# Part of an attention kernel's exponentials moved to VectorE, and some score matmuls made dense

## The chip, the cores and the metric

One core of a Trainium2 chip. The metric is the device time of one execution in microseconds (us), lower is better. Each run also has the mean clock that TensorE was granted, as a share of full speed, and a state: fast or slow (slow is over 1.5% above the fastest of the same kernel in its call). PE is TensorE, PEld its weight loads, DVE is VectorE, ACT is ScalarE, POOL is GpSimd.

## The reference, cut to what matters

Two independent layers on 2048 positions of width 448, 16 heads of 28, their outputs side by side.

```python
def _A_ref(x, wq, wk, wv, wo):          # first attention: all heads share one k and one v
    q = heads(x @ wq); k = x @ wk; v = x @ wv
    scores = einsum("bhqd,bkd->bhqk", q, k) * Dh ** -0.5
    return merge(einsum("bhqk,bkd->bhqd", softmax(scores), v)) @ wo
def _B_ref(x, wqkv, wo):                # second attention: each query sees 8 keys, 2 apart
    ...                                 # gather k and v at pos, pos-2, .. pos-14, softmax over 8
```

The first has 16 x 2048 x 2048 exponentials. The second has few, but many elementwise products.

## The kernel before: the parts that matter

A small scheduler in the program orders every instruction of each engine in advance from assumed durations; on the chip each engine gets its list in that order and waits on semaphores. The scores of the first attention come in 1024 units of one bank of PSUM, the memory that all 3821 matmuls in the trace of before write to (`ps`; 128 keys x 512 queries), four heads row-tiled in TensorE's array (the score matmuls of one batch start 3 ns apart there, in the median). ScalarE exponentiates them in batches of three and two banks in turn (`SLOTS`):

```python
for i, (sc, t, tb, j) in enumerate(us):                       # scores, 32 rows of the array each
    r = e.matmul(g.bank(b0 + i), g.kT[32*j:32*j+32, 128*tb:128*tb+128],
                 g.qT[32*j:32*j+32, sc % 2, t, :], start=True, stop=True, tile_position=(32*j, 0))
...
x = a("act", t_exp(w), lambda e, b0=b0, w=w, n=n: e.activation(
    g.expT[:, n % ERING, 0:w], g.ps[:, 512*b0:512*b0+w], ACT.Exp, scale=SCALE),
  R=[("ring", slot)], W=[("expT", n % ERING)], pr=-50)
...
for (sc, t, tb, j), r, i in grp:                              # value products, four units at a time
    x = e.matmul(g.bank(PVBANK, p0=32*j, p1=32*j+32), g.v_aug[:, tb, :],
                 g.expT[:, r, 512*i:512*i+512], start=tb == 0, stop=tb == 15, tile_position=(0, 32*j))
```

Sixteen key blocks of four heads (a "quad") accumulate in one bank; VectorE copies it out and normalises. The second attention runs in the gaps: its products on VectorE, its sums over TensorE. Where TensorE has had little dense work lately, by the scheduler's count (`area`), it puts matmuls on a tile of zeros ("fillers"): ahead of scores, ahead of small sums, or in idle time.

## Time and profile before

| | before |
|---|---|
| time, median of the first 3 executions | 502.77 us (500.17 to 507.64) |
| the profiled execution | 499.83 us, clock 0.996 |
| ScalarE busy | 476.4 us of 497.9 |
| VectorE busy | 237.6 us |
| exponentials | 205 of three banks, 204 of two, 1 of one |

The page and its groups are read in the prediction. What it tells but does not show is how the room on VectorE is spread. Busy time by stretch, before; the first columns are the stretch and its length, then each engine's busy us (count), last the granted clock, the share of the DMA engines and GB/s:

```profile
60.00:180.00 120.00, 116.07 (x988) 46.55 (x985) 64.16 (x118) 118.53 (x106) 3.40 (x5) 1.00 0.16 52
...
420.00:480.00 60.00, 57.16 (x448) 20.77 (x446) 18.48 (x35) 59.87 (x55) 1.23 (x2) 1.00 0.10 32
```

The third busy time, 64.16 of 120 us, is VectorE's: half busy in the middle, and less at the end.

### The profile page before, as it was taken

What the parts mean: (1) busy time and instruction counts of PE and PEld (TensorE: products, weight loads), DVE (VectorE), ACT (ScalarE), POOL (GpSimd) and SP (SyncE); (2) the same over time, 40 slices, a digit from 0 to 9 for tenths busy, and PEclk for the clock granted to TensorE, in tenths of its full rate; (3) what the DMA queues carried; (4) which work ended last, traced back from release to release, by engine and by line L of the source; (5) the groups of instructions that cost most, each with busy time, mean ns of one, the idle gap of its engine ahead of it and who ended that gap; (6) DMA issues with size and microseconds to landing.
All of it is one profiled execution on the core that took longest, in us unless ns stands there. A gap on an engine that the chain in (4) does not pass through costs nothing.

```text
span 497.9 us, 8754 instructions
## 1 busy us (share of the span) xinstructions
PE 477.7 (96%) x3821; PEld 185.1 (37%) x3821; DVE 237.6 (48%) x443; ACT 476.4 (96%) x431; POOL 25.3 (5%) x47
## 2 busy tenths in 40 slices
PE   8999999999989999999999999999999999999996
PEld 3433434343343334434343333434433343333322
DVE  3236448744463357454942495256722564037202
ACT  3989999999999999999999999999999999999994
POOL 8020000000000000000000000000000000000000
PEclk9989999999999999999999999999999999999999
DMA  7880220022003120302011302120020302020001
GB/s 158 146 229 2 84 73 13 18 84 84 1 11 108 34 73 11 93 0 84 1 41 62 121 2 67 37 66 19 20 84 18 103 11 94 0 84 1 20 0 38
DMA packets 41590, 27.35 MB, mean 55 GB/s; under 512 B 17058, under 2 KB 41040, under 8 KB 41552
## 3 DMA queue, kind: packets, MB, share of 16 engines
q1 hardware_dynamic: 39600, 25.65, 17.9%
q10 hardware_dynamic: 1776, 0.81, 0.6%
q8 instruction: 30, 0.49, 0.4%
q0 software_dynamic: 176, 0.33, 0.2%
q14 instruction: 8, 0.07, 0.0%
HBM read 17.60 MB, written 5.52 MB: 46 GB/s over the span
## 4 chain that ended last, share of the span: by engine, by line
ACT 62%; PE 31%; DVE 4%; DMA 1%; issue 1%; ACTq 0%
ACT expT L711 61%; PE ps L699 8%; PE ps L821 6%; PE ps L724 5%; PE ps L651 2%; PE ps L837 2%; DVE prod L915 2%; PE ps L697 1%; PE ps L749 1%; PE ps L926 1%; DMA wq<-in_A_wq_dram 1%; PE ps L933 1%; PE ps L780 1%; PE ps L665 1%; DVE a_n L902 1%
## 5 line engine op out<-in xcount | busy, mean ns | idle before, releaser
L711 ACT ACTIVATE expT<-ps 128x1536 bf16<-128x1536 f32 (+1 forms) x410 | 469.2, 1268 | 7.3 <-PE ps L699 6.0
L699 PE MATMUL ps<-qT,kT 32*128 32x512 bf16 x1024 | 160.2, 386 | 6.8 <-ACT expT L711 3.5
L724 PE MATMUL ps<-expT,v_aug 128*32 128x512 bf16 x1024 | 102.3, 390 | 0.4 <-DVE PV_sb L744 0.4
L699 PEld LDWEIGHTS ps<-qT,kT 32*128 32x128 bf16 x1024 | 39.3, 91 | 104.1 <-ACT expT L711 61.3
L724 PEld LDWEIGHTS ps<-expT,v_aug 128*32 128x32 bf16 x1024 | 26.2, 93 | 58.4 <-issue 55.9
L821 PE MATMUL ps<-xT_B,wqkv 128*112 128x512 bf16 (+1 forms) x128 | 44.9, 408 | 0.3 <-DVE qTB L827 0.3
L341 PE MATMUL ps<-warm 128*128 128x512 bf16 x140 | 42.9, 383 | 0.6 <-DVE rden L755 0.6
L862 DVE TENSOR_TENSOR stage<-qTB,kTB 112x1024 bf16<-112x1024 bf16 x64 | 41.5, 689 | 0.1
L915 DVE TENSOR_TENSOR prod<-Vsh,a_n 128x896 bf16<-128x896 bf16 x64 | 38.6, 658 | 0.0
L757 POOL COPY rrep<-rden 128x512 bf16<-128x512 bf16 x15 | 10.4, 695 | 419.0 <-DVE rden L755 419.0
L883 DVE TENSOR_REDUCE mx<-ps 128x16 f32<-128x128 f32 x15 | 4.4, 291 | 54.2 <-PE ps L871 54.2
L697 PE MATMUL ps<-warm 128*128 128x512 bf16 x69 | 25.7, 389 | 4.3 <-ACT expT L711 3.5
L871 PE MATMUL ps<-ones,stage 112*128 112x4 bf16 x512 | 28.2, 168 | 0.0
L871 PEld LDWEIGHTS ps<-ones,stage 112*128 112x128 bf16 x512 | 23.1, 96 | 13.3 <-issue 8.2
L926 PE MATMUL ps<-ident,padd 128*112 128x128 bf16 x256 | 25.5, 228 | 0.2
L364 PE MATMUL ps<-warm 128*128 128x384 bf16 x78 | 24.1, 328 | 0.5 <-DVE PV_sb L744 0.5
L926 PEld LDWEIGHTS ps<-ident,padd 128*112 128x112 bf16 x256 | 18.2, 129 | 12.1 <-issue 8.6
L821 PEld LDWEIGHTS ps<-xT_B,wqkv 128*112 128x112 bf16 (+1 forms) x128 | 14.4, 127 | 22.1 <-issue 18.9
L744 DVE COPY PV_sb<-ps 128x512 f32<-128x512 f32 x15 | 10.4, 691 | 25.2 <-PE ps L724 25.2
L651 PE MATMUL ps<-xT_A,wq 128*128 128x512 bf16 x64 | 20.9, 395 | 0.1
L755 DVE RECIPROCAL rden<-ps 128x16 bf16<-128x16 f32 x16 | 4.1, 253 | 34.3 <-PE ps L749 34.3
L749 PEld LDWEIGHTS ps<-sel,PV_sb 128*128 128x128 f32 x128 | 18.5, 190 | 5.1 <-issue 3.8
(97 smaller groups left out, 344.1 us busy)
## 6 DMA issues: line engine op xcount, KB each, us to landing
Vsh<-v_scratch SPq DMA_DIRECT2D x16, 896.0 KB, 4.6
v_scratch<-Vst SPq DMA_DIRECT2D x16, 112.0 KB, 1.7
out_dram<-outB SPq DMA_DIRECT2D x16, 112.0 KB, 1.7
out_dram<-outA SPq DMA_DIRECT2D x14, 112.0 KB, 1.7
wqkv<-in_B_wqkv_dram SPq DMA_DIRECT2D x1, 1008.0 KB, 5.6
stage<-in_A_x_dram ACTq DMA_DIRECT2D x1, 448.0 KB, 3.5
wo_B<-in_B_wo_dram SPq DMA_DIRECT2D x4, 98.0 KB
wo<-in_A_wo_dram SPq DMA_DIRECT2D x4, 98.0 KB
```

The costliest lines, as they stand in the source:

```text
L341: self.s.FILL = lambda b: (lambda e: e.matmul(self.bank(b), self.warm[:, 0:128], self.warm[:, :], start=True, stop=True))
L364: eng.matmul(self.bank(o.use.bank, 512 - lo, lo), self.warm[:, 0:128], self.warm[:, lo:512], start=True, stop=True)
L651: a("pe", t_mm(512), lambda e, u=u, t=t, kt=kt: e.matmul(g.bank(u.bank), g.wq4[64 * (kt // 3):, t, kt, :], g.xT_A[64 * (kt // 3):, kt, 512 ...
L697: e.matmul(g.bank(b0), g.warm[:, 0:128], g.warm[:, :], start=True, stop=True)
L699: r = e.matmul(g.bank(b0 + i), g.kT[32 * j:32 * j + 32, 128 * tb:128 * tb + 128], g.qT[32 * j:32 * j + 32, sc % 2, t, :], start=True, stop ...
L711: x = a("act", t_exp(w), lambda e, b0=b0, w=w, n=n: e.activation(g.expT[:, n % ERING, 0:w], g.ps[:, 512 * b0:512 * b0 + w], ACT.Exp, scale ...
L724: x = e.matmul(g.bank(PVBANK, p0=32 * j, p1=32 * j + 32), g.v_aug[:, tb, :], g.expT[:, r, 512 * i:512 * i + 512], start=tb == 0, stop=tb = ...
L821: a("pe", t_mm(512), lambda e, u=u, t=t, kt=kt, w=w: e.matmul(g.bank(u.bank, p1=KC), g.wqkv[64 * (kt // 3):, kt, w * D + KC * t:w * D + KC ...
L862: op = a("dve", t_dve_2x(1024), lambda e, t=t, qv=qv, kv=kv: e.tensor_tensor(out=g.prodT[0:KC, t, :, :], in0=qv, in1=kv, op=ALU.mult), R=R ...
L871: r = e.matmul(g.bank(u.bank, 128).rearrange("p (h w) -> p h w", w=WIN)[:, 4 * t:4 * t + 4, w], g.prodT[0:KC, t, w, :], g.ones4[:, :], sta ...
L915: a("dve", t_dve_2x(2 * D), lambda e, qr=qr, Vv=Vv, av=av: e.tensor_tensor(out=g.prod2[:, 2 * qr:2 * qr + 2, :].rearrange("p w (d h) -> p ...
L926: a("pe", 0.09, lambda e, u=u, t=t, w=w: e.matmul(g.bank(u.bank, 128, 128 * t, p1=KC), g.padd[:, w, KC * t:KC * t + KC], g.ident[:, :], st ...
```

## The change

Two parts with one aim each. First, of every sixth batch the last bank is not given to ScalarE: VectorE computes the exponential with a polynomial, up to a constant factor that a second, scaled copy of V takes out. Second, where TensorE's recent use is low by the scheduler's count, scores become matmuls over all 128 rows with a k that is zero outside the head's 32 rows: the array is kept busy with needed work in place of fillers. To make room in memory, buffers are shared and the ring of exponentials goes from 8 to 7 batches.

```diff
-ERING = 8
+ERING = 7
+OFF_EVERY, OFF_FROM, OFF_TO = 6, 28, 396
+    FULL = {2: 1500.0, 3: 1200.0}
+                elif (o.full and area(T) < self.FULL[o.full]
+                      and all(d.start is not None and d.end + self.LAT <= T for d in o.opt)):
+                    o.deps.update(o.opt)
+                    o.dur = 0.03 + 0.216 * o.full
+                    o.dense = 512 * o.full
 ...
+                    if box[0].full:
+                        r = e.matmul(g.bank(b0 + i), g.kz[:, j, 128 * tb:128 * tb + 128], g.qT[:, sc % 2, t, :], start=True, stop=True)
+                        continue
 ...
+            off = g.offload(n, us)
+            na = len(us) - off
-            w = 512 * len(us)
+            w = 512 * na
 ...
+            if off:
+                where.append((us[na],) + g.d_exp(b0 + na, slot) + (1,))
 ...
+        a("dve", t_dve_ps(512), lambda e: e.tensor_scalar(          # d_i: scores -> fixed point
+            out=ii, in0=g.bank(bank), scalar1=A2 * F, scalar2=-127 * F, op0=ALU.mult, op1=ALU.max), ...
+        a("dve", 0.4, lambda e: e.tensor_scalar(                    # d_e: exponent bits
+            out=ee, in0=hi, scalar1=127.0, scalar2=128.0, op0=ALU.add, op1=ALU.mult), ...
+        a("dve", t_dve_1x(512), lambda e: e.scalar_tensor_tensor(   # d_u, d_v, dexp: cubic in the fraction
+            out=uu, in0=lo, scalar=EP * F, in1=lo, op0=ALU.add, op1=ALU.mult), ...
```

Cuts are marked with dots, and the three comments are added here; two more such products follow the last one. Value products of one quad may now change places except for the first and last, the quad's sum has two buffers instead of four, and the scheduler's assumed paces were adjusted (`QT` 28.5 to 27, `BSTEP` 26 to 25), as were some of its assumed VectorE durations and the threshold for its idle fillers (`IDLE` 1400 to 1300).

More of the change, by code (lines that the diff above doesn't have):

```diff
@@ L32 @@
 WARM = 10
-QT = 28.5
+QT = 27.0
+ER, EP, EQ, E3 = 1.8383190070507454, 1.0590043062556727, 6.971225738216641, 0.078025670176921
+A2 = SCALE * 1.4426950408889634
+DVI = E3 * 2.0 ** -48
+OFF_EVERY, OFF_FROM, OFF_TO = 6, 28, 396
+DR = 4
 class Op:
@@ L38 @@
                  "kids", "start", "end", "seq", "waits", "signal", "count", "vc", "ninc", "claims", "idx",
-                 "dense", "fill")
+                 "dense", "fill", "full", "opt")
     def __init__(self, eng, dur, emit, pr, rel, name):
@@ L55, in __init__ @@
         self.fill = None
+        self.full = 0
+        self.opt = ()
 class Use:
@@ L75 @@
     WANT = 1200.0
-    IDLE = 1400.0
+    IDLE = 1300.0
+    FULL = {2: 1500.0, 3: 1200.0}
     FILL = None
@@ L218, in run @@
                     o.dense += 512 - o.use.spare
+                elif (o.full and area(T) < self.FULL[o.full]
[3 more added lines that the diff above has]
+                    o.dense = 512 * o.full
                 elif o.fill is not None:
+                    o.full = 0
                     o.fill = max(0, min(0 if waiting else 2, round((self.WANT - area(T)) * self.WIN / 512 + 0.3)))
@@ L309, in t_dve_1x @@
 def t_dve_1x(n):
-    return 0.09 + 1.04e-3 * n
+    return 0.16 + 1.04e-3 * n
 def t_dve_2x(n):
-    return 0.09 + 0.52e-3 * n
+    return 0.16 + 0.52e-3 * n
 def t_act(n):
@@ L405, in alloc @@
         self.stage = sb([128, 4096], BF16, "stage")
-        self.wqkv = sb([128, 4, 3 * D], BF16, "wqkv")
+        self.wqkv = sb([128, 4, 2 * D], BF16, "wqkv")
         self.wvB = sb([128, 4, D], BF16, "wvB")
@@ L409, in alloc @@
         self.wo4 = sb([128, 4, D], BF16, "wo4")
-        self.wq = sb([128, 4, D], BF16, "wq")
         self.wk = sb([128, 4, DH], BF16, "wk")
@@ L415, in alloc @@
         self.kT = sb([128, S], BF16, "kT")
-        self.k_sq = sb([128, 2, 512], BF16, "k_sq")
+        self.kz = sb([128, 4, S], BF16, "kz")
         self.q_sq = sb([128, 2, 512], BF16, "q_sq")
         self.qT = sb([128, 2, 4, 512], BF16, "qT")
-        self.v_aug = sb([128, 16, 32], BF16, "v_aug")
+        self.v_aug = sb([128, 2, 16, 32], BF16, "v_aug")
         self.expT = sb([128, ERING, EW], BF16, "expT")
-        self.PV_sb = sb([128, 4, 512], FP32, "PV_sb")
+        self.dexp = sb([128, DR, 512], BF16, "dexp")
+        self.d_i = sb([128, 2, 512], mybir.dt.int32, "d_i")
+        self.d_e = sb([128, 2, 512], mybir.dt.int16, "d_e")
+        self.d_u = sb([128, 1, 512], FP32, "d_u")
+        self.d_v = sb([128, 1, 512], FP32, "d_v")
+        self.PV_sb = sb([128, 2, 512], FP32, "PV_sb")
         self.oTn = sb([128, 4, 512], BF16, "oTn")
@@ L445, in alloc @@
         self.hq = sb([128, 3, 128], BF16, "hq")
-        self.cols = sb([128, 8], FP32, "cols")
+        self.cols = sb([128, 12], FP32, "cols")
         self.e30 = sb([32, 1], BF16, "e30")
-        self.gcol = sb([128, 16], FP32, "gcol")
+        self.gcol = sb([128, 2, 16], FP32, "gcol")
         self.warm = sb([128, 512], BF16, "warm")
         self.xst = self.stage[:, 0:4 * D].rearrange("p (b c) -> p b c", c=D)
+        self.k_sq = self.d_u[:, 0, :].bitcast(BF16).rearrange("p (t c) -> p t c", t=2)
+        self.wq = self.d_i[:, :, :].rearrange("p t c -> p (t c)").bitcast(BF16)[:, 0:4 * D].rearrange("p (t c) -> p t c", t=4)
+        self.wqv = self.Vsh[:, 1, 0:4, :]
         self.prodT = self.stage[:, :].rearrange("p (t w c) -> p t w c", t=4, w=WIN)
@@ L478, in consts @@
           R=["ident"], W=["qadd"], pr=-8)
+        a("dve", 0.2, lambda e: e.tensor_reduce(out=c[:, 8:12], in_=g.ident[:, :].rearrange("p (j e) -> p j e", e=32),
+                                                axis=AX.X, op=ALU.add), R=["ident"], W=["jmask"], pr=-1)
         a("act", 1.5, lambda e: e.activation(c[:, 7:8], g.warm[:, 0:1], ACT.Exp), R=["warm"], W=["c7"], pr=-10)
@@ L482, in consts @@
         a("gp", 0.1, lambda e: e.memset(g.wk[0:64, 3, :], 0.0), W=["wkz"], pr=-8.5)
-        a("gp", 0.2, lambda e: e.memset(g.wq[0:64, 3, :], 0.0), W=["wqz"], pr=-8.5)
+        a("gp", 0.2, lambda e: e.memset(g.wq[0:64, 3, :], 0.0), R=[("d_i", 0), ("d_i", 1)], W=["wqz"], pr=-8.5)
         a("gp", 1.6, lambda e: e.memset(g.wq4[:, 1:4, :, :], 0.0), W=[("wq4", 1), ("wq4", 2), ("wq4", 3)], pr=-8)
@@ L490, in consts @@
         a("dve", 0.1, lambda e: e.tensor_copy(out=g.e30[:, :], in_=g.ident[0:32, 30:31]), R=["ident"], W=["e30"], pr=-5)
-        a("dve", 0.1, lambda e: e.memset(g.v_aug[:, :, :], 0.0), W=["v_zero"], pr=-5)
+        a("dve", 0.1, lambda e: e.memset(g.v_aug[:, :, :, :], 0.0), W=["v_zero"], pr=-5)
         a("dve", 0.1, lambda e: e.tensor_copy(out=g.sel4[:, :], in_=iv[:, 28, :]), R=["ident"], W=["sel4"], pr=30, rel=15)
@@ L517, in loads @@
         a("act", 1.0, wload(g.wk, g.A_wk, 0, DH), W=["wk"], dsem="i_wk", land=3, pr=-20, ninc=2)
-        a("act", 1.0, wload(g.wq, g.A_wq, 0, KC), W=[("wq", 0)], dsem="i_wq0", land=3, pr=-19, ninc=2)
+        a("act", 1.0, wload(g.wq, g.A_wq, 0, KC), R=[("d_i", 0), ("d_i", 1)], W=[("wq", 0)], dsem="i_wq0", land=3, pr=-19, ninc=2)
         a("gp", 1.5, wload(g.wv, g.A_wv, 0, DH), W=["wv"], dsem="i_wv", land=4, pr=-7.5, ninc=2)
-        a("gp", 1.5, wload(g.wq, g.A_wq, KC, D), W=[("wq", 1)], dsem="i_wq", land=4, pr=-7.5, ninc=2)
+        a("gp", 1.5, wload(g.wq, g.A_wq, KC, D), R=[("d_i", 0), ("d_i", 1)], W=[("wq", 1)], dsem="i_wq", land=4, pr=-7.5, ninc=2)
         for c in range(1, NCH):
@@ L530, in loads @@
         a("sp", 1.2, lambda e: [
-            e.dma_start(out=g.wqkv[:, 0:3, :], in_=g.B_wqkv[0:384, :].rearrange("(t p) c -> p t c", p=128)),
-            e.dma_start(out=g.wqkv[64:128, 3, :], in_=g.B_wqkv[384:448, :])],
-          W=["wqkv"], dsem="i_wb", land=8, pr=1, rel=4, ninc=2)
+            e.dma_start(out=g.wqkv[:, 0:3, :], in_=g.B_wqkv[0:384, 0:2 * D].rearrange("(t p) c -> p t c", p=128)),
+            e.dma_start(out=g.wqkv[64:128, 3, :], in_=g.B_wqkv[384:448, 0:2 * D]),
+            e.dma_start(out=g.wqv[:, 0:3, :], in_=g.B_wqkv[0:384, 2 * D:].rearrange("(t p) c -> p t c", p=128)),
+            e.dma_start(out=g.wqv[64:128, 3, :], in_=g.B_wqkv[384:448, 2 * D:])],
+          W=["wqkv", ("Vsh", 1)], dsem="i_wb", land=8, pr=1, rel=4, ninc=4)
         a("sp", 1.5, lambda e: [e.dma_start(
@@ L549, in loads @@
                 in_=g.wq[:, :, KC * t:KC * t + KC].rearrange("p k (j d) -> p k j d", d=DH)),
-              R=[("wq", min(t, 1)), "wqz"], W=[("wq4", t)], pr=-6 + t)
+              R=[("wq", min(t, 1)), "wqz", ("d_i", 0), ("d_i", 1)], W=[("wq4", t)], pr=-6 + t)
         for kt in range(4):
@@ L553, in loads @@
                 out=g.wvB[64 * (kt // 3):, kt, :].rearrange("p (d h) -> p d h", h=H),
-                in_=g.wqkv[64 * (kt // 3):, kt, 2 * D:3 * D].rearrange("p (h d) -> p d h", d=DH)), R=["wqkv"], W=[("wvB", kt)], pr=3)
+                in_=g.wqv[64 * (kt // 3):, kt, :].rearrange("p (h d) -> p d h", d=DH)), R=[("Vsh", 1)], W=[("wvB", kt)], pr=3)
     HB = (0, 1, 2, 3, 4)
@@ L560, in a_head @@
         g, a = self, self.s.add
+        g.kz_ops = {}
         for i in range(WARM):
@@ L593, in a_head @@
                 a("act", t_act(512), lambda e, u=u, ksq=ksq: e.activation(ksq, g.bank(u.bank), ACT.Square),
-                  R=[u], W=[("k_sq", c % 2)], use=u, pr=-100)
+                  R=[u, "d_u"], W=[("k_sq", c % 2)], use=u, pr=-100)
             else:
@@ L599, in a_head @@
                 a("dve", t_dve_2x(512), lambda e, ksq=ksq, kc=kc: e.tensor_tensor(out=ksq, in0=kc, in1=kc, op=ALU.mult),
-                  R=[("kT", c)], W=[("k_sq", c % 2)], pr=pr)
+                  R=[("kT", c), "d_u"], W=[("k_sq", c % 2)], pr=pr)
             a("pe", t_mm(512), lambda e, u=u, ksq=ksq: e.matmul(g.bank(u.bank), g.hq[:, 2, :], ksq, start=False, stop=True, skip_group_check=True),
-              R=[("k_sq", c % 2), "hq"], W=[u], use=u, pr=pr, dense=512)
+              R=[("k_sq", c % 2), "hq", "d_u"], W=[u], use=u, pr=pr, dense=512)
             kc = g.kT[:, 512 * c:512 * c + 512]
@@ L606, in a_head @@
               R=["kadd"], W=[("kT", c)], use=u, pr=pr)
+            g.kz_ops[c] = [
+                a("gp", 0.8, lambda e, j=j, c=c, kc=kc: e.tensor_scalar(
+                    out=g.kz[:, j, 512 * c:512 * c + 512], in0=kc, scalar1=g.cols[:, 8 + j:9 + j], scalar2=0.0,
+                    op0=ALU.mult, op1=ALU.add), R=["jmask", ("kT", c)], W=[("kz", c)], pr=2 + c) for j in range(4)]
             if c == 0:
@@ L627, in a_v @@
               R=[("kT", c), "e30"], W=[u], use=u, pr=pr)
-        gc = g.gcol[:, 4 * c:4 * c + 4]
-        a("act", 0.2, lambda e, u=u, gc=gc: e.activation(gc, g.bank(u.bank, 4, 128), ACT.Exp, scale=SCALE),
+        gc, gd = g.gcol[:, 0, 4 * c:4 * c + 4], g.gcol[:, 1, 4 * c:4 * c + 4]
+        a("act", 0.2, lambda e, u=u: e.activation(gc, g.bank(u.bank, 4, 128), ACT.Exp, scale=SCALE),
           W=[("gcol", c)], use=u, pr=-100)
-        a("gp", 0.2, lambda e, gc=gc: e.tensor_copy(out=g.v_aug[:, 4 * c:4 * c + 4, DH:DH + 1], in_=gc.unsqueeze(2)),
-          R=[("gcol", c), "v_zero"], W=[("v_aug1", c)], pr=-3)
-        a("dve", t_dve_ps(112), lambda e, u=u, gc=gc: e.tensor_tensor(
-            out=g.v_aug[:, 4 * c:4 * c + 4, 0:DH], in0=g.bank(u.bank, 128).rearrange("p (t c) -> p t c", c=32)[:, :, 0:DH],
-            in1=gc.unsqueeze(2).to_broadcast([128, 4, DH]), op=ALU.mult),
-          R=[("gcol", c), "v_zero"], W=[("v_aug", c)], use=u, pr=pr)
+        a("gp", 0.2, lambda e: e.tensor_scalar(out=gd, in0=gc, scalar1=DVI, scalar2=0.0, op0=ALU.mult, op1=ALU.add),
+          R=[("gcol", c)], W=[("gd", c)], pr=-2)
+        for w, gg in enumerate((gc, gd)):
+            k = ("gd" if w else "gcol", c)
+            a("gp", 0.2, lambda e, w=w, gg=gg: e.tensor_copy(out=g.v_aug[:, w, 4 * c:4 * c + 4, DH:DH + 1], in_=gg.unsqueeze(2)),
+              R=[k, "v_zero"], W=[("v_aug1", w, c)], pr=-3 + w)
+            a("dve", t_dve_ps(112), lambda e, u=u, w=w, gg=gg: e.tensor_tensor(
+                out=g.v_aug[:, w, 4 * c:4 * c + 4, 0:DH],
+                in0=g.bank(u.bank, 128).rearrange("p (t c) -> p t c", c=32)[:, :, 0:DH],
+                in1=gg.unsqueeze(2).to_broadcast([128, 4, DH]), op=ALU.mult),
+              R=[k, "v_zero"], W=[("v_aug", w, c)], use=u, pr=pr + w)
     def a_q(self, sc, first=False):
@@ L683, in a_loop @@
         g.last_exp = {}
+        g.nd = 0
         n, pos, where = -1, 0, []
@@ L705, in a_loop @@
             box.append(o)
+            o.full = len(us) if len(us) > 1 else 0
+            o.opt = {x for (_, _, tb, _) in us for x in g.kz_ops[tb // 4]}
             o.fill = 0
@@ L713, in a_loop @@
               R=[("ring", slot)], W=[("expT", n % ERING)], pr=-50)
-            for i in range(len(us)):
+            for i in range(na):
                 g.last_exp[b0 + i] = x
-            for i, x in enumerate(us):
-                where.append((x, n % ERING, i))
+                where.append((us[i], ("expT", n % ERING), g.expT[:, n % ERING, 512 * i:512 * i + 512], 0))
+            if off:
+                where.append((us[na],) + g.d_exp(b0 + na, slot) + (1,))
             while len(where) >= 4 or (where and pos == NU):
@@ L722, in pv @@
                 def pv(e, grp=grp):
-                    for (sc, t, tb, j), r, i in grp:
-                        x = e.matmul(g.bank(PVBANK, p0=32 * j, p1=32 * j + 32), g.v_aug[:, tb, :],
-                                     g.expT[:, r, 512 * i:512 * i + 512], start=tb == 0, stop=tb == 15,
-                                     tile_position=(0, 32 * j))
-                    return x
-                o = a("pe", 0.33, pv, R=[("expT", r) for r in sorted({y[1] for y in grp})] + [("v_aug", tb // 4), ("v_aug1", tb // 4)], W=["pv"], pr=-40,
-                      dense=700)
+                    for (sc, t, tb, j), _, src, w in grp:
+                        x = e.matmul(g.bank(PVBANK, p0=32 * j, p1=32 * j + 32), g.v_aug[:, w, tb, :], src,
+                                     start=tb == 0, stop=tb == 15, tile_position=(0, 32 * j))
+                    return x
+                o = a("pe", 0.33, pv, R=sorted({y[1] for y in grp}) + [(k, w, tb // 4) for k in ("v_aug", "v_aug1") for w in sorted({y[3] for y in grp})],
+                      W=["pv"] if tb in (0, 15) else [], pr=-40, dense=700)
+                if tb == 0:
+                    quad = [o]
+                elif tb < 15:
+                    o.deps.add(quad[0])
+                    quad.append(o)
+                else:
+                    o.deps.update(quad)
                 if pv_first:
@@ L734, in a_loop, with offload, d_exp @@
                     g.a_quad_end(sc, t)
+    def offload(self, n, us):
+        return int(n % OFF_EVERY == 0 and OFF_FROM <= n <= OFF_TO and 0 < us[-1][2] < 14)
+    def d_exp(self, bank, slot):
+        g, a = self, self.s.add
+        m = g.nd
+        g.nd += 1
+        h = m % 2
+        ii, ee, uu, vv, out = g.d_i[:, h, :], g.d_e[:, h, :], g.d_u[:, 0, :], g.d_v[:, 0, :], g.dexp[:, m % DR, :]
+        lo = ii.bitcast(mybir.dt.uint16).rearrange("p (c two) -> p c two", two=2)[:, :, 0]
+        hi = ii.bitcast(mybir.dt.int16).rearrange("p (c two) -> p c two", two=2)[:, :, 1]
+        F = 65536.0
+        a("dve", t_dve_ps(512), lambda e: e.tensor_scalar(
+            out=ii, in0=g.bank(bank), scalar1=A2 * F, scalar2=-127 * F, op0=ALU.mult, op1=ALU.max),
+          R=[("ring", slot)], W=[("d_i", h)], pr=-45)
+        a("dve", 0.4, lambda e: e.tensor_scalar(out=ee, in0=hi, scalar1=127.0, scalar2=128.0, op0=ALU.add, op1=ALU.mult),
+          R=[("d_i", h)], W=[("d_e", h)], pr=-0.5)
+        a("dve", t_dve_1x(512), lambda e: e.scalar_tensor_tensor(
+            out=uu, in0=lo, scalar=EP * F, in1=lo, op0=ALU.add, op1=ALU.mult), R=[("d_i", h)], W=["d_u"], pr=-0.5)
+        a("dve", t_dve_1x(512), lambda e: e.scalar_tensor_tensor(
+            out=vv, in0=lo, scalar=ER * F, in1=ee.bitcast(BF16), op0=ALU.add, op1=ALU.mult),
+          R=[("d_i", h), ("d_e", h)], W=["d_v"], pr=-0.5)
+        a("dve", t_dve_1x(512), lambda e: e.scalar_tensor_tensor(
+            out=out, in0=uu, scalar=EQ * F * F, in1=vv, op0=ALU.add, op1=ALU.mult),
+          R=["d_u", "d_v"], W=[("dexp", m % DR)], pr=-0.5)
+        return ("dexp", m % DR), out
     def a_quad_end(self, sc, t):
@@ L740, in a_quad_end @@
         if last:
-            a("act", t_act(512), lambda e: e.activation(g.PV_sb[:, t, :], g.bank(PVBANK), ACT.Copy),
-              R=["pv"], W=[("PV", t, 0), ("PV", t, 1)], pr=-30)
-        else:
-            a("dve", t_dve_ps(512), lambda e: e.tensor_copy(out=g.PV_sb[:, t, :], in_=g.bank(PVBANK)),
-              R=["pv"], W=[("PV", t, 0), ("PV", t, 1)], pr=-30)
+            a("act", t_act(512), lambda e: e.activation(g.PV_sb[:, t % 2, :], g.bank(PVBANK), ACT.Copy),
+              R=["pv"], W=[("PV", t % 2, 0), ("PV", t % 2, 1)], pr=-30)
+        else:
+            a("dve", t_dve_ps(512), lambda e: e.tensor_copy(out=g.PV_sb[:, t % 2, :], in_=g.bank(PVBANK)),
+              R=["pv"], W=[("PV", t % 2, 0), ("PV", t % 2, 1)], pr=-30)
         pr = -35 if last else end + 20
@@ L749, in a_quad_end @@
             a("pe", 0.25, lambda e, u=u, s4=s4: e.matmul(
-                g.bank(u.bank, 4, 4 * s4), g.PV_sb[:, t, 128 * s4:128 * s4 + 128], g.sel4[:, :], start=True, stop=True),
-              R=[("PV", t, s4 // 2), "sel4"], W=[u], use=u, pr=pr)
+                g.bank(u.bank, 4, 4 * s4), g.PV_sb[:, t % 2, 128 * s4:128 * s4 + 128], g.sel4[:, :], start=True, stop=True),
+              R=[("PV", t % 2, s4 // 2), "sel4"], W=[u], use=u, pr=pr)
         def rec(e, u=u):
@@ L768, in a_quad_end @@
             a("dve", t_dve_ps(sl.stop - sl.start), lambda e, u=u, sl=sl: e.tensor_tensor(
-                out=g.oTn[:, t, sl], in0=g.PV_sb[:, t, sl], in1=g.bank(u.bank)[:, sl], op=ALU.mult),
-              R=[("PV", t, 0), ("PV", t, 1)], W=[("oTn", t, hf)] if last else [("oTn", t, 0), ("oTn", t, 1)], use=u, pr=-1)
+                out=g.oTn[:, t, sl], in0=g.PV_sb[:, t % 2, sl], in1=g.bank(u.bank)[:, sl], op=ALU.mult),
+              R=[("PV", t % 2, 0), ("PV", t % 2, 1)], W=[("oTn", t, hf)] if last else [("oTn", t, 0), ("oTn", t, 1)], use=u, pr=-1)
         if t < 3:
@@ L796 @@
     B0 = 34.0
-    BSTEP = 26.0
+    BSTEP = 25.0
     def b_all(self):
@@ L901, in b_soft @@
         for b in range(2):
-            a("dve", t_dve_1x(128), lambda e, b=b: e.tensor_tensor(
+            a("dve", 0.62, lambda e, b=b: e.tensor_tensor(
                 out=g.a_n[:, par, b].rearrange("p w h -> p h w"), in0=g.e_t[:, par, b],
```

## The prediction

> **What bounds the kernel now.** I read the page's first two parts, then the chain of waits, then the groups by form, the list of waits and some stretches. The page:
>
> ```profile
> PE 477.7 (96%) x3821; PEld 185.1 (37%) x3821; DVE 237.6 (48%) x443; ACT 476.4 (96%) x431; POOL 25.3 (5%) x47
> ...
> DVE  3236448744463357454942495256722564037202
> ACT  3989999999999999999999999999999999999994
> ...
> PEclk9989999999999999999999999999999999999999
> ...
> ACT 62%; PE 31%; DVE 4%; DMA 1%; issue 1%; ACTq 0%
> ```
>
> ScalarE and TensorE both read 96%, so the share alone decides nothing. TensorE's is inflated: part of it is matmuls on a tile of zeros, there only to keep the array busy (140 + 69 + 78 of them). VectorE is half empty; the clock is full. The groups by form:
>
> ```profile
> L711 ACT ACTIVATE expT<-ps 128x1536 bf16<-128x1536 f32 x205 | 303.3, 1479 | 6.8 <-PE ps L699 5.6
> L711 ACT ACTIVATE expT<-ps 128x1024 bf16<-128x1024 f32 x204 | 215.8, 1058 | 0.5 <-PE ps L699 0.5
> ...
> L341 PE MATMUL ps<-warm 128*128 128x512 bf16 x140 | 42.9, 383 | 0.6 <-DVE rden L755 0.6
> ...
> L744 DVE COPY PV_sb<-ps 128x512 f32<-128x512 f32 x15 | 10.4, 691 | 25.2 <-PE ps L724 25.2
> ...
> L768 DVE TENSOR_TENSOR oTn<-PV_sb,ps 128x512 bf16<-128x512 f32 x15 | 10.2, 683 | 13.1 <-PE ps L763 13.1
> ...
> L663 DVE TENSOR_TENSOR q_sq<-qT 128x512 bf16<-128x512 bf16 x15 | 6.9, 457 | 0.4
> ```
>
> The exponentials wait in all some 7 us for scores. They start at 12.3 us and end by 490.2, so ScalarE is filled end to end and its stream sets the time. The chain in order of time gives its pitch where nothing disturbs it:
>
> ```profile
> 155.88 27.39 ACT expT L711 x24
> ```
>
> Twelve pairs of a three-bank and a two-bank batch in 27.39 us: 2.283 us a pair; 205 pairs are 468 us, against 478 from the first exponential to the end of the last. So there are only about 10 us of anything else between. And who waits for whom:
>
> ```profile
> PEld ps L699 <- ACT expT L711: 61.3, 173, 0.7
> ...
> ACT expT L711 <- PE ps L699: 6.0, 19, 0.7
> ```
>
> TensorE's score loads wait 61 us for ScalarE to free banks, ScalarE waits 6 us for TensorE: ScalarE is the bound, TensorE follows.
>
> [...]
>
> **The change, part by part.**
>
> ScalarE. Every sixth batch from the 28th to the 396th, unless its last key block is 0, 14 or 15, keeps two of its three banks on ScalarE. The built order has 51 such cases: 154 wide and 255 two-bank exponentials in place of 205 and 204. The third bank's worth is the difference of the two forms, (1479 − 1058) = 421 ns[...]. 51 × 0.427 = 21.8 us off the stream that sets the end. Nothing is added on ScalarE.
>
> VectorE. Each case adds five operations on 128x512: PSUM scores scaled to int32 with a clamp (as the PSUM copy, 0.69), the exponent from the upper 16 bits (0.43 [...]), and three fp32 products of the polynomial (0.69 each, as oTn). That is 3.19 us × 51 = 163 us, so VectorE goes from 238 to about 400 of some 480 us, 83%. Between two neighbouring first steps (six batches, 3 × 2.283 − 0.427 = 6.42 us of ScalarE) the built VectorE order holds 6.1 to 6.9 us of durations; back-to-back independent operations overlap by 5 to 10% (64 products of 689 ns are 44.1 us by sum, 41.5 by busy time), so 5.7 to 6.4 us. VectorE is therefore nearly full through the middle. About one offload in six is skipped, which lets it catch up.
>
> Waits. The offloaded bank's value product on TensorE stands five batches after its scores in 33 of 51 cases, 4 to 8 in the rest: five batches are 5.4 us. VectorE's own work from first to last step, summed from the durations of before, is 3.8 to 5.5 us in most cases, up to 8.2 where the lag is eight batches. Lag less work is 0.5 us in the median, and negative (to −1.1 us) in 5 cases. That margin is thin, as TensorE executes in order: a late result holds up the next scores and then ScalarE. The value products otherwise commute now (only the first and last of a quad are ordered), and the ring of exponentials falls from 8 to 7 batches, still 7.5 us deep. The first step must also free its bank: 0.69 us plus what is in progress on VectorE, beside 0.93 us of ScalarE on the other two banks, so mostly hidden.
>
> TensorE. 127 score batches (290 matmuls) become dense with the zero-padded k: three at 0.22 us take 0.65 instead of 0.32 tiled, two take 0.43. That adds 290 × 0.216 − 127 × 0.32 = 22 us of array time. Out go 103 idle fillers, 64 fillers ahead of scores and 24 partial ones: 103 × 0.22 + 64 × 0.32 + 24 × 0.17 = 47 us. TensorE is relieved by some 25 us, nearly all off the path; I give it 0 to 2 us (fewer of ScalarE's 6 us of waits), and expect no change of clock.
>
> Start and tail. GpSimd makes 16 zero-padded k slices (about 0.7 us each by its 128x512 copy at 695 ns) while it idles in the first 40 us; weights share buffers with later scratch. The first exponential should still come at about 12 us and the tail from 490 us keep its 8 us. 0.
>
> Sum: 502.8 − 21.8 = 481.0. New waits by the tight VectorE and the in-order TensorE: I allow 3 to 4 us, half of the 7 us that ScalarE waits today, since 46 of 51 cases have margin. Against that, two of the four known executions of before (500.17 and 499.83) are 2.7 us below the median. I put it at 483, 3.9% less.
>
> **The rivals.**
>
> First: VectorE becomes the bound. If the exponent step runs at 0.69, or strided 16-bit reads cost more, VectorE gets 13 us more work, each period 6.0 to 6.7 us against 6.42, and there is no slack left. For it: six of the forty slices already read 7 or more tenths on VectorE, and 4.8 us of its work stands in a typical lag of 5.4 us. Against: the tail from 420 us on has VectorE at 31% (18.5 of 60 us), so lateness of the second attention's work can run into it, and the order takes first steps ahead of most work. It would give back 8 to 15 us: 489 to 497.
>
> Second: TensorE takes ScalarE's place. Dense scores take twice as long and start only when a bank is free; a three-bank one (0.65 us plus 0.23 of waiting) must hide behind a two-bank exponential of 0.93. 36 batches are of that kind; if each exposed 0.2 us, 7 us would be lost: 488. Against: they stand only where TensorE had little to do, where the fillers' 0.32 us was paid just as well.
>
> Third: a full gain with a bonus. If fewer fillers and fewer tiling changes also remove most of the 6 us of waits: 476 to 478.
>
> Slower by 2% needs 32 us of new waits, 0.6 us in every case.
>
> **Range and chances.** Most likely 483; 476 (gain plus bonus from a fast run of before) to 492 (the first rival at half its size) should hold it 8 times in 10. The 2% line lies at 492.7, so 10 of the 19.8 us between would have to be lost: faster 0.86, same 0.12, slower 0.02.
>
> **What would show it.** Exponentials: 154 and 255, pitch of an offload period near 6.42 us, ScalarE busy near 455 us and still over 94% of the span. VectorE busy 375 to 400 us. The five new groups at 0.69, 0.43 and three times 0.69 us. Value products that read VectorE's result should show waits for it of under 5 us in all, and ScalarE's waits for scores under 12 us. The prediction is wrong if the product steps take over 0.9 us, if VectorE's share passes 90% in the middle, if ScalarE's idle time exceeds 15 us, or if the clock falls.

The figures it rests on, as the trace of before has them: from the start of one exponential to the next it is 1330 ns at the shortest for three banks and 903 for two, so the third bank is worth 0.427 us; `q_sq` takes 0.425 us in the median, which is the 0.43 taken for the exponent step; the copy out of PSUM takes 691 ns and the fp32 product 683 (the groups above). A filler of 512 columns starts 0.217 us after the one before it (median); row-tiled scores start 0.322 us after the filler put ahead of them, and value products behind scores 0.315 us after the last of these (medians). VectorE's durations sum to 261.9 us for 237.6 busy, an overlap of 9%. That VectorE can read its bank at the usual pace while ScalarE reads the other two was an assumption of mine; in the trace of the changed kernel 50 of the 51 first steps lie wholly within exponentials, and these took 692 ns in the mean.

## The result, and the profile after

| | before | changed |
|---|---|---|
| median of 4 executions | 505.19 us | 482.77 us |
| lowest, highest | 500.17, 507.64 | 482.35, 485.64 |
| ScalarE busy | 476.4 us | 457.4 us |
| VectorE busy | 237.6 us | 378.6 us |
| TensorE busy | 477.7 us | 456.6 us |

The ratio of the fast runs is 0.9576 (95% interval 0.9496 to 0.9656). Ratios here are the mean time of one kernel's fast runs over that of the other's in the same rounds, so not quite the ratio of the medians; a fifth execution of the changed kernel, 482.25 us, is in it. The result is right against the reference.

The page of the changed kernel:

```profile
PE 456.6 (94%) x3630; PEld 177.3 (37%) x3630; DVE 378.6 (78%) x703; ACT 457.4 (95%) x431; POOL 40.7 (8%) x71
...
DVE  4325787998869888889878988788968989888673
ACT  3789999999999999999999998999999999999993
...
PEclk9699999999999999999999999999999999999999
```

and one stretch of it, to set beside the first line of the table of stretches before:

```profile
60.00:180.00 120.00, 115.79 (x942) 45.16 (x941) 102.46 (x187) 118.21 (x112) 4.49 (x5) 1.00 0.14 45
```

ScalarE is still filled end to end; VectorE has gone from half empty to mostly 8 or 9 tenths in the middle of the forty slices (102.46 of 120 us here). This execution lost clock in its second slice: it is the 485.64 us one, and the others, at a clock of 0.999 to 1.0, took 482.2 to 482.9. The groups by form:

```profile
L756 ACT ACTIVATE expT<-ps 128x1024 bf16<-128x1024 f32 x255 | 258.9, 1065 | 4.9 <-PE ps L770 3.2 <-PE ps L740 1.0 <-PE ps L738 0.2
L756 ACT ACTIVATE expT<-ps 128x1536 bf16<-128x1536 f32 x154 | 229.2, 1488 | 6.7 <-PE ps L740 5.1 <-PE ps L738 0.9
...
L807 DVE SCALAR_TENSOR_TENSOR d_u<-d_i 128x512 f32<-128x512 uint16 x51 | 36.0, 706 | 0.0
L802 DVE TENSOR_SCALAR d_i<-ps 128x512 int32<-128x512 f32 x51 | 35.3, 692 | 14.3 <-PE ps L740 13.1 <-PE ps L738 0.7
L809 DVE SCALAR_TENSOR_TENSOR d_v<-d_i,d_e 128x512 f32<-128x512 uint16 x51 | 35.2, 690 | 0.0
L812 DVE SCALAR_TENSOR_TENSOR dexp<-d_u,d_v 128x512 bf16<-128x512 f32 x51 | 34.8, 682 | 0.0
...
L805 DVE TENSOR_SCALAR d_e<-d_i 128x512 int16<-128x512 int16 x51 | 21.6, 423 | 0.2
```

The counts 255 and 154 are the moved banks; the five new groups took 692, 423, 706, 690 and 682 ns. The chain in order of time and the list of waits:

```profile
90.82 25.69 ACT expT L756 x24
```

```profile
ACT expT L756 <- PE ps L740: 6.2, 15, 1.2
...
ACT expT L756 <- PE ps L770: 3.2, 3, 1.6
```

Twelve pairs in 25.69 us where they took 27.39: 1.70 us less, four banks at 0.427. The second waiting row is new: three long waits, 3.2 us in all, of an exponential on a value product (L770). An exponential needs its ring buffer back, and a value product that stands behind a late VectorE result has not read it yet (in this trace TensorE's matmuls start in the order of the built list, but for one place near the start). Two runs below have the ring of 7 but not these five steps (the dense scores alone, and VectorE's work taken out), and neither has such a row; so the shorter ring alone does not make it.

Where the time went is clearest between two executions without loss of clock to speak of: the profile before (clock 0.996, 497.9 us) and one of the changed kernel at 1.0 (481.0 us, run again below). From the first exponential's start to the last one's end: 477.2 us before, 459.1 after, 18.1 less. The start is 0.6 us later and the tail 0.7 us longer. So 51 x 0.427 = 21.8 us came off ScalarE, and about 5 us came back as waits, start and tail.

### The profile page after: what moved, and what is told of

Its sections match the earlier page's. It is cut to its first block, busy times and chain, and to the rows that moved or that the text cites. A ratio compares the mean times of both kernels' runs of the same rounds, so it can differ in the third digit from the quotient of the medians.

```text
span 483.8 us, 8734 instructions
## 1 busy us (share of the span) xinstructions
PE 456.6 (94%) x3630; PEld 177.3 (37%) x3630; DVE 378.6 (78%) x703; ACT 457.4 (95%) x431; POOL 40.7 (8%) x71
## 4 chain that ended last, share of the span: by engine, by line
ACT 62%; PE 35%; DVE 1%; DMA 1%; ACTq 0%; issue 0%; DVEq 0%
ACT expT L756 62%; PE ps L740 7%; PE ps L902 6%; PE ps L770 6%; PE ps L738 4%; PE ps L688 2%; PE ps L918 2%; PE ps L830 1%; PE ps L1014 1%; PE ps L615 1%; DMA d_i<-in_A_wq_dram 1%; PE ps L651 1%; PE ps L861 1%; PE ps L1007 1%; PE ps L702 0%; PE ps L380 0%
## 5 line engine op out<-in xcount | busy, mean ns | idle before, releaser
L756 ACT ACTIVATE expT<-ps 128x1024 bf16<-128x1024 f32 (+1 forms) x410 | 450.2, 1223 | 11.6 <-PE ps L740 6.2
L740 PE MATMUL ps<-qT,kT 32*128 32x512 bf16 x734 | 111.3, 388 | 12.4 <-ACT expT L756 9.7
L770 PE MATMUL ps<-expT,v_aug 128*32 128x512 bf16 x973 | 98.7, 393 | 0.1
L738 PE MATMUL ps<-qT,kz 128*128 128x512 bf16 x290 | 84.5, 384 | 8.8 <-ACT expT L756 6.9
L740 PEld LDWEIGHTS ps<-qT,kT 32*128 32x128 bf16 x734 | 27.2, 91 | 82.1 <-ACT expT L756 58.4
L770 PEld LDWEIGHTS ps<-expT,v_aug 128*32 128x32 bf16 x973 | 24.1, 93 | 63.6 <-issue 57.8
L802 DVE TENSOR_SCALAR d_i<-ps 128x512 int32<-128x512 f32 x51 | 35.3, 692 | 14.3 <-PE ps L740 13.1
L807 DVE SCALAR_TENSOR_TENSOR d_u<-d_i 128x512 f32<-128x512 uint16 x51 | 36.0, 706 | 0.0
L809 DVE SCALAR_TENSOR_TENSOR d_v<-d_i,d_e 128x512 f32<-128x512 uint16 x51 | 35.2, 690 | 0.0
L812 DVE SCALAR_TENSOR_TENSOR dexp<-d_u,d_v 128x512 bf16<-128x512 f32 x51 | 34.8, 682 | 0.0
L738 PEld LDWEIGHTS ps<-qT,kz 128*128 128x128 bf16 x290 | 19.3, 99 | 35.2 <-ACT expT L756 28.3
L805 DVE TENSOR_SCALAR d_e<-d_i 128x512 int16<-128x512 int16 x51 | 21.6, 423 | 0.2
```

Source lines behind the costliest of these rows:

```text
L738: r = e.matmul(g.bank(b0 + i), g.kz[:, j, 128 * tb:128 * tb + 128], g.qT[:, sc % 2, t, :], start=True, stop=True)
L740: r = e.matmul(g.bank(b0 + i), g.kT[32 * j:32 * j + 32, 128 * tb:128 * tb + 128], g.qT[32 * j:32 * j + 32, sc % 2, t, :], start=True, stop ...
L770: x = e.matmul(g.bank(PVBANK, p0=32 * j, p1=32 * j + 32), g.v_aug[:, w, tb, :], src, start=tb == 0, stop=tb == 15, tile_position=(0, 32 * j))
L802: a("dve", t_dve_ps(512), lambda e: e.tensor_scalar(out=ii, in0=g.bank(bank), scalar1=A2 * F, scalar2=-127 * F, op0=ALU.mult, op1=ALU.max) ...
L807: a("dve", t_dve_1x(512), lambda e: e.scalar_tensor_tensor(out=uu, in0=lo, scalar=EP * F, in1=lo, op0=ALU.add, op1=ALU.mult), R=[("d_i", h ...
L809: a("dve", t_dve_1x(512), lambda e: e.scalar_tensor_tensor(out=vv, in0=lo, scalar=ER * F, in1=ee.bitcast(BF16), op0=ALU.add, op1=ALU.mult) ...
```

## The experiments

The theory to test: the gain is the 51 banks off ScalarE, less what a nearly full VectorE gives back; dense scores do nothing on the path. Rivals: the dense scores carry part of the gain, or cost part of it; VectorE is already the bound.

### The changed kernel again, and its two parts apart

No edit for the first. The other three share the same chip and the same runs of the kernel before.

> The changed kernel once more, as the yardstick of the runs beside it. Every theory: ratio to the kernel before 0.95 to 0.966, about 482.5 us.

Measured: 482.66 us median (482.27 to 485.6), clock 0.989 to 1.0. The kernel before, in the same rounds: 498.34 us at a clock of 0.999, then 500.21, 500.23, 501.53 at 0.990 to 0.993, and 507.64 (clock 0.972), 532.6 (0.916) and 550.92 (0.876). The ratio of fast runs is 0.9665, with an interval from 0.9604 to 0.9727. The exponentials of this execution:

```profile
L756 ACT ACTIVATE expT<-ps 128x1024 bf16<-128x1024 f32 (+1 forms) x410 | 449.7, 1221 | 8.7 <-PE ps L740 3.3
```

Their idle time is 8.7 us against 7.3 before, only 1.4 more. The rest of the 3.7 us between 21.8 and 18.1 hides in the durations: their means are 1487 and 1063 ns here, 1479 and 1058 before; 154 x 8 + 255 x 5 ns is 2.5 us. A wait shorter than the overlap of two neighbours (0.115 us in the median behind a two-bank exponential, before) is not idle time on the page. By the starts in the trace of before, the shortest distance from a two-bank exponential to the next is 903 ns (77 of them have it) and the mean 978: some 15 us over the shortest, of which the idle column has 6. That leaves about 9 us of short waits outside it, an estimate, and by the same count about 11 in this execution of the changed kernel.

The offload without the dense scores:

```diff
-    FULL = {2: 1500.0, 3: 1200.0}
+    FULL = {2: 0.0, 3: 0.0}
```

> The offloaded exponentials without the dense scores (all scores row-tiled, fillers put back by the scheduler). My theory (the gain is 51 x 0.427 us off ScalarE; dense scores only relieve an engine off the path): within 2 us of the changed kernel, 481 to 485 us, clock as before. Rival (the dense scores are needed to gain, because TensorE with tiled scores, fillers and a shorter ScalarE stream becomes the bound or loses its clock): 488 us or more, with more than 20 us of ScalarE's idle time on scores.

Measured: 480.53 us at a clock of 1.0, then 494.68, 495.3 and 501.95 at 0.958, 0.958 and 0.945. In its one execution at full clock the theory holds: the offload alone gives all of it, 2 us more than the whole change even. But three of four executions lost clock, which no execution of the changed kernel did to that extent. The rival was half right: the clock.

The dense scores without the offload:

```diff
-        return int(n % OFF_EVERY == 0 and OFF_FROM <= n <= OFF_TO and 0 < us[-1][2] < 14)
+        return 0
-QT = 27.0
+QT = 28.5
```

(with `BSTEP` back at 26.)

> The dense scores without the offload (schedule constants of the kernel before). My theory: ScalarE has its full 410 batches, so the time of the kernel before, 498 to 505 us, ratio 0.99 to 1.0, at most 2 us better by fewer waits for scores. Rival (the gain comes in good part from TensorE): under 494 us.

Measured: 501.32 to 501.92 us, clock 0.996 to 1.0 in all four. It is 3 us slower than before at full clock (498.34), no different from before's median (501.53), and has none of its bad executions.

Neither part: both edits.

> Neither part, but the rest of the change (ring of 7, value products that commute, two instead of four buffers for the quad's sum, new scheduler constants). My theory: within 1% of the kernel before. Rival (the small changes carry or cost something): outside 498 to 507 us.

Measured: 503.26 (clock 0.990), 507.26 (0.975), 511.94 (0.963) and 531.69 us (0.917). The rest of the change brings no gain; whether it costs a microsecond or two can't be told, as no execution had full clock. Two of the four lie outside the expected 498 to 507 us, both with the lowest clocks. Its profile fell in the slowest, and shows what such an execution is. The page, ScalarE and the clock by slice, then two stretches (columns as above):

```profile
ACT  3766555799999999999999999999999999999994
...
PEclk9555555699999999999999999999999999999999
```

```profile
60.00:80.00 20.00, 20.00 (x70) 4.77 (x69) 6.85 (x10) 11.70 (x10) 0.00 (x0) 0.50 0.16 53
...
100.00:120.00 20.00, 19.12 (x165) 7.65 (x163) 13.64 (x26) 19.07 (x19) 0.61 (x1) 0.98 0.16 52
```

From 15 to 101 us the clock is at half. TensorE is busy all of the 20 us and does 70 matmuls, where the later stretch at full clock has 165 (of another mix, so the counts are no rate); ScalarE is busy 11.7 of 20 us and waits for scores 34.1 us in the whole execution: there TensorE is the bound. Busy time as the profile counts it does not by itself bring the full clock: 20.00 of 20 us, and still 0.50. What does is not shown by this trace.

### TensorE with needed work only

```diff
-    FULL = {2: 1500.0, 3: 1200.0}
+    FULL = {2: 0.0, 3: 0.0}
-    WANT = 1200.0
+    WANT = 0.0
-    IDLE = 1300.0
+    IDLE = 0.0
```

> The offload with neither dense scores nor fillers of any kind after the start, so TensorE does only needed work, scores row-tiled. If zero-padded scores and fillers only cost time: 476 to 480 us. If they are what keeps the granted clock up: long stretches at a clock of 0.5 in every execution, above 520 us, with ScalarE waiting for scores there.

Measured: 597.42 to 618.44 us, clock 0.61 to 0.65, in every execution. The clock by slice and ScalarE's wait for scores:

```profile
PEclk9555555555555575755595786999555855555557
```

```profile
ACT expT L756 <- PE ps L740: 117.5, 162, 2.2
```

So the useless work is what holds the clock (0.61 to 0.65 without it, 0.945 to 1.0 in the offload alone with its fillers), and the clock holds ScalarE's supply (117.5 us of waits for scores against 6.2 + 1.1 = 7.3 in the changed kernel; a row-tiled score matmul takes 545 ns in the mean against 388). Fillers alone (the kernel before, and the offload alone) do it in some executions; with dense scores it held in nearly all. Over these experiments the kernel before had a clock under 0.985 in 12 of 22 executions. The nine kernels with dense scores run here had it under 0.985 in 1 of 36. This is the second part's real worth: it does not make the fast execution faster, it makes the slow ones rare. Why dense scores hold it better is not shown: the changed kernel has 290 of them and 96 fillers (by its trace, the 10 at the start not counted), the offload alone 222 fillers, the kernel before 287, and amount and placing were not varied apart.

### Are the three-bank dense scores what costs 2 us?

```diff
-    FULL = {2: 1500.0, 3: 1200.0}
+    FULL = {2: 1500.0, 3: 0.0}
```

> Dense scores only for the two-bank batches; the 36 three-bank ones go back to tiled scores. If the 2 to 3 us by which the changed kernel at full clock is slower than the offload alone come from three-bank dense scores (0.65 us to hide behind a 0.90 us exponential): 480 to 481 us, clock 0.99 or more in every execution. If they come from elsewhere: 482 to 484 us. If the three-bank ones are needed to hold the clock: executions above 485 us.

Measured: 483.08 to 483.6 us, clock 0.998 to 1.0. No better than the changed kernel, so the three-bank ones are not the cost, nor are they needed for the clock. The scheduler makes another order of everything with each such edit, and 2 us is within what an order can move. Building the kept kernels again, without a chip, gives the end that the scheduler itself planned (its `self.span`): 469.1 us for the changed kernel, 466.2 for the offload alone, and 486.1 for the dense scores alone against 482.9 before. So both differences at full clock (2 us for the one, 3 us for the other) stand in the planned orders already, as far as a plan tells: this run's plan, 468.3, is 0.9 us under the changed kernel's, and the run was 0.8 over it.

### VectorE: nothing, more, and still more

The polynomial taken out; the value product reads a tile of ones, so the result is wrong (the scaled V makes these terms next to nothing; with 5% of the softmax terms dropped the result still passed the comparison):

```diff
-        a("dve", ...)   # the five steps
+        a("dve", 0.6, lambda e: e.memset(g.dexp[:, :, :], 1.0), W=[("dexp", r) for r in range(DR)], pr=5)   # once
```

> As the changed kernel, but the five VectorE steps of the offload are gone: the third bank is simply not exponentiated and the value product reads a tile of ones (a wrong result on purpose). If VectorE's added work costs nothing, the time is that of the changed kernel, 481 to 484 us. If its late results are what keeps the gain 4 to 5 us under 21.8, the time is 476 to 479 us.

Measured: 479.58 to 480.18 us, median 479.96, 2.7 us under the changed kernel: between the two expectations, about half way. VectorE's busy time is 137 us below the changed kernel's:

```profile
PE 452.9 (95%) x3603; PEld 176.8 (37%) x3603; DVE 242.0 (51%) x449; ACT 457.9 (96%) x431; POOL 39.5 (8%) x71
```

So that work cost 2.7 us, about half of the 5 us that came back. Here too the planned end is earlier, 466.1 us against 469.1, so the 2.7 us are the work with the order that it brings.

One product step done twice in each case:

```diff
         a("dve", t_dve_1x(512), lambda e: e.scalar_tensor_tensor(
             out=vv, in0=lo, scalar=ER * F, in1=ee.bitcast(BF16), op0=ALU.add, op1=ALU.mult), ...)
+        a("dve", t_dve_1x(512), lambda e: e.scalar_tensor_tensor(   # the same again
+            out=vv, in0=lo, scalar=ER * F, in1=ee.bitcast(BF16), op0=ALU.add, op1=ALU.mult), ...)
```

> One of the 0.69 us product steps is done twice in each of the 51 cases (35 us more VectorE work, right result). VectorE stands at 86% in the middle of the changed kernel, so 0.69 us more in 6.4 us makes 96%. If VectorE has the room that its share shows: within 2 us of the changed kernel. If a nearly full in-order VectorE is the next bound: 486 us or more, with value products waiting on its last step for over 5 us.

Measured: 514.18 to 515.15 us, clock 0.993 to 0.995: 32 us more for 51 x 0.69 = 35 us of work. The changed kernel stands at the edge, and beyond it VectorE's work goes to the time nearly one to one, with VectorE at 86% of the middle, not 100%. A stretch of it, the waits, then one of them in order of time:

```profile
60.00:180.00 120.00, 112.56 (x871) 43.05 (x870) 103.66 (x187) 111.52 (x104) 4.51 (x5) 1.00 0.13 43
```

```profile
ACT expT L756 <- PE ps L770: 27.4, 16, 4.1
```

```profile
294.53 0.68 DVE L802 TENSOR_SCALAR d_i<-ps 128x512 int32<-128x512 f32 x1
...
301.66 0.68 DVE L815 SCALAR_TENSOR_TENSOR dexp<-d_u,d_v 128x512 bf16<-128x512 f32 x1
...
302.74 0.39 PE L770 MATMUL ps<-dexp,v_aug 128*32 128x512 bf16 x1
...
303.18 7.39 ACT L756 ACTIVATE expT<-ps 128x1024 bf16<-128x1024 f32 x7 [2.36 <-PE ps L770]
```

Between the first step and the last lie 7.8 us, as other VectorE work stands between in the list. TensorE comes to the value product at 302.74, and only after it can ScalarE go on, 2.36 us late. TensorE's own wait for `dexp` before a value product's load is short in all runs (0.4 us in the changed kernel, 1.6 here, 3.9 at most, where the clock was 0.61), so the sign that I had expected, over 5 us there, did not come; the row to watch is ScalarE's wait for L770, two steps further. Besides the 16 long waits (27.4 us), the tail from the last exponential to the end is 17.3 us, 8 more than in the changed kernel.

One rival is open. The scheduler's plan for this run ends at 503.5 us, 34 later than for the changed kernel, so the loss is in the order that it built. It built that order with VectorE slower than it is (416.8 us planned for the changed kernel, 378.6 measured). The edge at 86% is therefore that of this scheduler's orders; that no other order would do better is not shown.

More offloads, every fifth batch:

```diff
-OFF_EVERY, OFF_FROM, OFF_TO = 6, 28, 396
+OFF_EVERY, OFF_FROM, OFF_TO = 5, 28, 396
```

(`QT` 26.8, `BSTEP` 24.8.)

> Every fifth batch: 61 offloads, 10 x 0.427 = 4.3 us less on ScalarE and 32 us more VectorE work (about what the extra step added, but with more ScalarE time taken away). If ScalarE still sets the time: 478 to 480 us. If VectorE is at its limit, as the extra step says: 500 us or more, with ScalarE waiting in few, long waits (over 1 us) on value products.

Measured: 504.87 to 505.06 us, clock 0.988 to 0.990. The planned end is late here too (492.9 us). VectorE's limit, as expected, but most of it shows in another place than the long waits that I had named (7.4 us on value products). The exponentials end at 479.4 us, 7 us later than in the changed kernel; then comes this:

```profile
474.21 5.21 ACT L756 ACTIVATE expT<-ps 128x1024 bf16<-128x1024 f32 x5
...
487.42 2.42 DVE L996 TENSOR_TENSOR prod<-Vsh,a_n 128x896 bf16<-128x896 bf16 x4
...
500.29 0.62 DVE L1017 CAST outB<-ps 128x448 bf16<-128x448 f32 x1 [1.77 <-PE ps L1014]
```

The second attention's last two blocks have slipped behind the exponentials and run alone, one engine after the other, for 24 us. Lateness of work with low priority costs nothing until it reaches the end. The run changes one thing more: with an odd step 31 of the 61 offloads fall on two-bank batches and leave exponentials of one bank (175 of three banks, 203 of two, 32 of one in its trace), so it is not only more of the same.

Half as many, every twelfth batch (`OFF_EVERY` 12, `QT` 27.8, `BSTEP` 25.5):

> Every twelfth batch in place of every sixth: 26 offloads instead of 51, 25 x 0.427 = 10.7 us more on ScalarE, about 80 us less VectorE work. If each offload is worth its 0.427 us: 491 to 494 us. If the offloads at the tight places of VectorE give back part of their worth (2.7 us in all by the run without VectorE work): 490 to 491.5 us.

Measured: 491.79 and 491.85 us at a clock of 0.998 to 1.0, 494.15 and 495.07 in executions with a later start or less clock. From 26 to 51 offloads the best time falls by 9.5 us, 0.38 us each, against 0.427 of ScalarE: the second half of the offloads gives back a tenth, 1.2 of 10.7 us, which is within what an order can move.

### Two tries at a better kernel

Half of the second attention's adds to GpSimd:

```diff
-            a("dve", t_dve_2x(2 * D), lambda e, hf=hf: e.tensor_tensor(
+            a("gp" if hf else "dve", 2.0 if hf else t_dve_2x(2 * D), lambda e, hf=hf: e.tensor_tensor(
```

> One of each two adds of the second attention (16 of 32, 0.62 us each on VectorE, 10 us in all) goes to GpSimd, which is idle after 40 us. If relief of VectorE recovers its share of the 2.7 us that its added work costs: 480 to 482 us. If GpSimd's adds hinder VectorE's own two-tensor steps, or come too late: 484 us or more, with longer means of those steps.

Measured: 484.36 and 484.49 us at a clock of 0.999, 486.4 and 489.21 at 0.993 and 0.989 (in the profiled 489.21 the exponentials also start 3 us late); about 2 us slower than the changed kernel, as the second expectation had it. VectorE's remaining steps got longer, and the group of GpSimd shows the price there:

```profile
L943 DVE TENSOR_TENSOR stage<-qTB,kTB 112x1024 bf16<-112x1024 bf16 x64 | 48.2, 770 | 2.7 <-PE ps L952 2.7
L996 DVE TENSOR_TENSOR prod<-Vsh,a_n 128x896 bf16<-128x896 bf16 x64 | 41.6, 679 | 0.0
...
L1000 POOL TENSOR_TENSOR padd<-prod 128x896 bf16<-128x896 bf16 x16 | 36.4, 2276 | 168.8 <-DVE prod L996 157.6 <-PE ps L1007 11.0 <-DVE d_i L802 0.2
```

The means are 770 and 679 ns against 706 and 626 in the changed kernel: 64 x 64 + 64 x 53 ns is 7.5 us, most of the 10 us relief. An add took 2276 ns on GpSimd, against 616 on VectorE in the changed kernel. Why VectorE's steps are longer in this run is not shown.

Offloads from the 10th batch on (`OFF_FROM` 10), two more:

> Offloads from the 10th batch on instead of the 28th, 53 in all, as VectorE is half empty before 60 us. Two more at 0.427 us: 481.5 to 482.2 us if nothing else moves; above 483 us if the start's other VectorE work collides with them.

Measured: 481.31, 481.35 and 481.73 us at a clock of 0.996 to 1.0, and one execution of 491.77 at 0.976. The three are about 1 us under the changed kernel's (measured in another call), as two banks at 0.427 would make; with one execution in four at low clock it is no proven improvement.

Two others were not run: every fourth batch (the scheduler found no end) and a ring of 8 (no room in memory).

## Why the prediction was right or wrong

The time (483 against 482.77) and the direction were right. One reading is a little off without consequence: the last exponential before ends at 489.5 us in the trace, not 490.2. By steps:

- **ScalarE is the bound, and 51 x 0.427 us come off it.** Right: 154 and 255 exponentials, the undisturbed stretch in exact agreement (25.69 us), and without VectorE's work the time is 480.0 us.
- **The five VectorE steps at 0.69, 0.43 and three times 0.69.** Right within 3%; VectorE busy 378.6 us in the range of 375 to 400, 85% of the middle (102.46 of 120 us).
- **New waits of 3 to 4 us.** Too small: about 5 us between the two traces and 5.7 between the fastest executions (21.8 less the 16.1 from 498.34 to 482.27), of which VectorE's work makes 2.7. The way was the predicted one, through the in-order TensorE and the ring.
- **The clock: "expect no change", 0 to 2 us for the dense scores.** This step failed. The 25 us of relief for TensorE came (477.7 to 452.5 us busy in the second trace), but at full clock it brings nothing (the offload alone has the fastest execution with a right result among the parts, 480.53 us), and without them the clock falls in most executions. I had read a clock of 0.996 in one execution as a property of the kernel.
- **The baseline, 502.8 less half of 2.7 us.** Too high by 3 us for an execution at full clock (498.34), which about offset the waits that I had set too small, so part of the exactness of 483 is luck. The median of 505.19 in the comparison contains lost clock: of the 22.4 us between the medians, 16 are there at full clock (498.34 to 482.27) and about 6 are clock that the kernel before loses (the clocks of those four were not recorded, but in the later calls every execution from 507.3 to 507.9 us had 0.972 to 0.978).
- **The first rival (VectorE becomes the bound)** did not happen, but was close: 0.69 us more in each case, and the whole gain is gone (ratio to before 1.019). I had put 8 to 15 us on 13 us more work, about one to one, and the extra step measured that: 32 us for 35.
- **The second rival (three-bank dense scores)**: not seen; without them the time is the same. **The third** (fewer waits than before): not seen.

## What to carry to other kernels

Work taken off a full engine counts one to one only while the engine that receives it can take it in its own order: here, in the orders that this scheduler builds, it was at its limit at 86% busy in the middle, and 10% more work cost all of the gain. Look at the planned end before you blame the chip for a change's cost: the order can have it already. Look for the limit two steps downstream (the ring that is not freed) and at the end (low-priority work that slips behind the last of the main stream). And a clock read in one execution is a sample: before calling filler work useless, see how many executions keep the clock without it.
